# A spectral mixer and MLP on one core: staging places, conversion slots and output buffers changed

## The chip, the cores and the metric

The kernel runs on one core of a Trainium2 chip. The metric is the device time of one execution in microseconds (us), the median of three runs. Engines are called TensorE (PE in the rows, with its weight loads as PEld), VectorE (DVE), ScalarE (ACT), GpSimd (POOL) and SyncE (SP, which issues nearly all DMAs here).

## What is computed

Eight sequences of 3072 tokens with 256 channels go through a real FFT along the sequence, a complex 256 x 256 mix with bias, a soft threshold of 0.01 and the inverse FFT, and then through an MLP with 2048 hidden units and a softplus.

```python
X = np.fft.rfft(x, axis=1)
Yr = Xr @ w_r - Xi @ w_i + b_r
Yi = Xr @ w_i + Xi @ w_r + b_i
Yr = np.sign(Yr) * np.maximum(np.abs(Yr) - 0.01, 0.0)     # Yi the same
y = np.fft.irfft(Y, n=3072, axis=1)
h = y.reshape(-1, 256) @ w_in
g = np.maximum(h, 0.0) + np.log1p(np.exp(-np.abs(h)))
out = g @ w_out
```

Matrix products are made of three: each operand is split into a high part and a remainder, and high x high, high x remainder and remainder x high are summed. The MLP weights arrive as 64-bit numbers and are converted on the chip.

## The kernel before

**Order.** Everything is issued in an order that the program writes out itself (`manual_schedule`). The end of the function is a planner and a loop over slots. `product(i, f, ...)` puts one step of the spectral part into the first free slot from i on, `at(i, f, ...)` puts DMA issues and small work into slot i, `before` holds the weight conversions, whose pieces go one to a slot. In each slot the loop emits, in this order: the first half of the MLP's products (`slot_products`), one piece of each running conversion, the spectral step, the `at` list, whatever was put off in the slot before (`later`: stores and remainders), and the second half of the products (`slot_second`). Each engine runs its own instructions strictly in that order. A tile that is asked for when all buffers of its tag hold tiles in use makes its first writer wait for one of them.

**Slots.** Slots -64 to -1 are the fill: the whole spectral part of batch 0, up to its first pair of token blocks. From slot 0 on, four slots make one key (b, bp, mp): batch, pair of token blocks (three to a batch), and one of eight double tiles of the hidden units. Eight keys, 32 slots, make a pair; 768 slots in all. A plain slot has twelve matmuls and takes 2.72 us with nothing waiting, the third of each four nine and 2.04. Into these slots go the spectral steps of the batches to come: s1 (0.69 us of TensorE), s3 (0.91), mix (2.17), s4 (0.68), s5 (1.37). `add(key, C11, "e")` and `add(key, C21, "e")` on VectorE free the PSUM bank "e" that the first matmul of the next slot's `pse` group overwrites.

**Turns.** Only the first two pairs (0,0) and (0,1) take turns: each runs half of its hidden units (slots 0 to 15 and 16 to 31), puts its sums into DRAM (`part_dr`), and comes back for the other half (32 to 47 and 48 to 63) so that there is time to convert the second half of the weights. `load_part` brings the sums back. In a pair's last but one and last steps (the second and third slot after its 32, called e+1 and e+2 with e the next pair's first slot) `ffn2` copies four [128 x 512] results from PSUM into `ot` tiles: block j=1 in e+1, block j=0 in e+2, each with k=0 on ScalarE and k=1 on VectorE, and stores them one slot later. When partial sums are added, VectorE makes all four.

**Buffers in question.** Tag "ot" (2 buffers) holds the four results and, during conversions, the work tile `u`. Tag "d" (2 buffers) holds the results of s4 on their way to DRAM (`s4`, line 434, stored one slot later). "r0" and "r1" hold the raw tokens of s5. "dp" (4) holds s5's inputs and early raw weights; "w64" (1) later raw weights; "wp" (1) the converted weights before they are stored to DRAM, from where `stream_w` reads them for each key.

**Conversions.** Sixteen of them (w_in and w_out by turns, eight double tiles). Six start in the fill ("ahead", their adds on GpSimd), in slots -42 to -7, seven slots apart; the others start in slots 0, 3, 6, 10, ... 34.

Of the kernel before, what the change touches and what calls it, by code (L numbers as in the profile page):

```python
# [10 lines left out]
F32 = mybir.dt.float32  # L11
F32R = mybir.dt.float32r
# [5 lines left out]
P = 128  # L18
N1, N2 = 96, 32
NG = 24  # L20
NP = NG // 2
BLK = 512
# [11 lines left out]
def tile_spectral_mixer_mlp(ctx, tc, x, w_r, w_i, bias, bias_0, w_in, w_out, f, f_hi, f_lo, g1, g3, g3_hi, g3_lo, hm, out):  # L34
# [14 lines left out]
    sb = ctx.enter_context(tc.tile_pool(name="sb", bufs=2))  # L49
# [23 lines left out]
    w_1 = y1[:, 10 * 512:].bitcast(F32R)  # L73
# [23 lines left out]
    def store(dst, src, what, eng=None):  # L97

        def start():
            (eng or nc.sync).dma_start(dst, src)  # L100
            stored[what] += 1

        later.append(start)
# [32 lines left out]

    def load_w(which, m2):

        if m2 < 3:
            st = sb.tile([P, 1024 + 4 * N1], F32, tag="dp", name="w64", bufs=4)[:, :1024]  # L140
        else:
            st = sb.tile([P, 1024], F32, tag="w64", name="w64", bufs=1)
        nc.sync.dma_start(st.rearrange("p (a n) -> p a n", a=2).bitcast(U32), (w_in if which else w_out)[:, m2])
        stages[which, m2] = st

    def split_w(which, m2):

        st = stages.pop((which, m2)).bitcast(U32).rearrange("p (n w) -> p n w", w=2)
        lw, hw = st[:, :, 0], st[:, :, 1]
        t = sb.tile([P, 512], F32, tag="t", name="wt", bufs=5)
        u = sb.tile([P, 512], F32, tag="ot", name="wu")
        ti, ui = t.bitcast(U32), u.bitcast(U32)
        v, g = nc.vector, nc.gpsimd
        nc.scalar.activation(u, hw.bitcast(F32), AF.Square)
        v.tensor_scalar(out=ti, in0=hw, scalar1=3, scalar2=0x3FFFFFF8, op0=ALU.logical_shift_left, op1=ALU.bitwise_and)
        v.scalar_tensor_tensor(out=ti, in0=hw, scalar=0xC0000000, in1=ti, op0=ALU.bitwise_and, op1=ALU.bitwise_or)  # L160
        nc.scalar.mul(lw.bitcast(F32), lw, 2.0 ** -52)
        yield
        v.scalar_tensor_tensor(out=t, in0=u, scalar=2.0 ** -30, in1=t, op0=ALU.is_ge, op1=ALU.mult)
        v.tensor_scalar(out=ui, in0=ti, scalar1=0xFF800000, scalar2=None, op0=ALU.bitwise_and)
        g.tensor_tensor(out=u, in0=lw.bitcast(F32), in1=u, op=ALU.mult)
        yield
        n = 7 * P if which else 2 * D
        w = w_1 if early and which else sb.tile([P, 2 * 7 * P], F32R, tag="wp", name="wp", bufs=1)
        w = w[:, :2 * n]
        hi, lo, src = w[:, :n], w[:, n:], w[:, n:].bitcast(F32)  # L170
        ahead = bool(early)
        e = g if ahead else v
        if which:

            tm, um = [a.rearrange("p (k m n) -> p m k n", k=2, m=2) for a in (t, u)]
            a21 = tm[:, 1, 0]
            o = [src[:, i * P:(i + 1) * P] for i in range(7)]
            e.tensor_tensor(out=src[:, A11 * P:(A11 + 2) * P].rearrange("p (k n) -> p k n", k=2), in0=tm[:, 0], in1=um[:, 0], op=ALU.add)
            e.tensor_tensor(out=a21, in0=a21, in1=um[:, 1, 0], op=ALU.add)
            e.tensor_tensor(out=o[A22], in0=tm[:, 1, 1], in1=um[:, 1, 1], op=ALU.add)  # L180
        else:
            e.tensor_tensor(out=src, in0=t, in1=u, op=ALU.add)
        if ahead:
            yield
            yield
        if which:
            v.tensor_tensor(out=o[S1], in0=a21, in1=o[A22], op=ALU.add)
            v.tensor_tensor(out=o[S3], in0=o[A11], in1=a21, op=ALU.subtract)
            v.tensor_tensor(out=o[S2], in0=o[S1], in1=o[A11], op=ALU.subtract)
            v.tensor_tensor(out=o[S4], in0=o[A12], in1=o[S2], op=ALU.subtract)  # L190
        yield
        nc.scalar.copy(hi, src)
        yield
        v.tensor_tensor(out=lo, in0=src, in1=hi.bitcast(F32), op=ALU.subtract)
        yield
        nc.sync.dma_start((w1_dr if which else w2_dr)[m2][:, :], w.bitcast(F32))
        stored["w", which, m2] += 1
# [10 lines left out]
    def mm3(ps, wh, wl, xh, xl, start, stop, more=False):  # L208
        nc.tensor.matmul(ps, wh, xh, start=start, stop=False, skip_group_check=more)  # L209
        nc.tensor.matmul(ps, wh, xl, start=False, stop=False, skip_group_check=more)  # L210
        nc.tensor.matmul(ps, wl, xh, start=False, stop=stop, skip_group_check=more)  # L211
# [10 lines left out]
    early = [None]  # L222
# [376 lines left out]
    def load_part(blk):  # L599
        partial[blk] = []  # L600
        for k in range(2):
            assert stored["part", blk, k] == 1
            t = sb.tile([P, BLK], F32, name="part", **(dict(tag="d") if blk % 2 else dict(tag=f"r{k}", bufs=1)))
            nc.sync.dma_start(t, part_dr[blk, k][:, :])
            partial[blk].append(t)

    def ffn2(key, what, first, last):
        b, bp, mp = key
        m, j = divmod(what, 2)
        blk = 2 * bp + j  # L610
        if first:
            po[b, blk] = [ps_o.tile([P, BLK], F32, tag="o", name="pso") for _ in range(2)]
        wt = w_t[0, key].rearrange("p (h n) -> p h n", h=2)
        gh, gl = gt.pop((key, what))
        for k in range(2):
            w = slice(m * D + k * P, m * D + k * P + P)
            mm3(po[b, blk][k], wt[:, 0, w], wt[:, 1, w], gh, gl, first, last)
        if last:
            o = po.pop((b, blk))
            for k in range(2):  # L620
                ot = sb.tile([P, BLK], F32, tag="ot", name="ot")
                if blk in partial and not b:
                    nc.vector.tensor_tensor(out=ot, in0=o[k], in1=partial[blk][k], op=ALU.add)
                elif k == 0:
                    nc.scalar.copy(ot, o[k])
                else:
                    nc.vector.tensor_copy(ot, o[k])
                if mp == NM // 2 - 1:
                    store(out[b, blk, k], ot, "out")
                else:  # L630
                    part_dr[blk, k] = dram.tile([P, BLK], F32, tag=f"part{blk}{k}", name="part_dr", bufs=1)
                    store(part_dr[blk, k][:, :], ot, ("part", blk, k))
# [51 lines left out]
    with tc.manual_schedule():  # L684
# [7 lines left out]
        def at(i, f, *args):  # L692
            fill.setdefault(int(i), []).append((f, args))

        def product(i, f, *args):
            i = int(i)
            while i in steps:
                i += 1
            steps[i] = f, args
            return i  # L700

        def plan_s1(b, start, step, first=0):
            for c in range(first, 16):
                t = product(start + step * (c - first), s1, b, c)
                at(t - 3, split_x, b, c)
                at(t - (5 if b == 1 else 7), load_x, b, c)

        def plan_mix(b, start, step):
            mixed = done = start
            for gp in range(NP):  # L710
                t = product(max(start + step * gp, mixed), s3, b, gp)
                at(max(t - 4, 14), load_a, b, gp)
                mixed = product(max(t + (3 if gp else 4), done + 1), mix, b, gp)
                done = product(mixed + (3 if b == 1 else 4), s4, b, gp)

        def plan_s5(b, bp, start):

# [21 lines left out]
        t0 = -len(first)  # L739
# [18 lines left out]
            at(t0 + 14 + k, load_mix, k)  # L758
            at(t0 + 18 + k, split_mix, k)
        for j in range(NM):  # L760
            t = t0 + 22 + 7 * j if j < 6 else 3 * (j - 6) if j < 8 else 6 + 4 * (j - 8)
            at(t - (6 if j < 6 else 8 if j < 7 else 2), load_w, (j + 1) % 2, j // 2)
            before.setdefault(t, []).append(split_w((j + 1) % 2, j // 2))
        last = first.index(("s4", 0, NP - 1)) + t0
        for c in need_d(0):
# [6 lines left out]
            at(6 + 2 * k, combine_mix, 1 + k)  # L772

        nt = NT
        plan_s1(1, 0, 1.6, 8)
        for b in range(B):
            for bp in range(1, NPAIR):
                plan_s5(b, bp, nt * b + (NM if (b, bp) == (0, 1) else 2 * NM * bp) - 14)
            if b + 1 < B:
                plan_mix(b + 1, *((16, 4.9) if b == 0 else (nt * b - 4, 5.6)))  # L780
                plan_s5(b + 1, 0, nt * (b + 1) - 14)
        for b in range(2, B):
            plan_s1(b, *((16, 4.4) if b == 2 else (nt * (b - 2) - 4, 5.4)))
# [2 lines left out]
        for bp in range(2):  # L786
            t = 4 * keys.index((0, bp, NM // 2 - 1))
            at(t + 4, load_part, 2 * bp + 1)
            at(t + 5, load_part, 2 * bp)
        for i, key in enumerate(keys):  # L790
            if i:
                at(4 * i - 4, stream_w, 1, key[2], key)
# [5 lines left out]
        for i in range(min([*fill, *steps]), nt * B + 3):  # L798
# [8 lines left out]
            if i in steps:  # L807
                f, args = steps.pop(i)
# [108 lines left out]
```

## Time and profile before

| | us |
|---|---|
| median of three runs (2702.85 to 2706.63) | 2703.62 |
| the profiled execution | 2708.39 |
| its span, from first to last instruction | 2706.2 |
| TensorE busy in the span | 2616.3 (97%) |
| VectorE, ScalarE, GpSimd busy | 1635.0, 1725.3, 298.0 |

Where slots begin in this trace, found by counting the groups of six `pso` matmuls that end each slot:

| slot | begins at us | slot | begins at us |
|---|---|---|---|
| 0 | 124.4 | 40 | 324.0 |
| 12 | 196.7 | 52 | 366.0 |
| 21 | 238.75 | 53 | 377.1 |
| 36 | 297.7 | 76 | 474.5 |

A busy TensorE is no measure of speed by itself, since its clock has two levels; the granted clock stands beside the busy time (1.00 is the full 2.4 GHz, 0.50 is 1.2 GHz). Idle time in brackets is that of the engine just before the instruction, with what ended it.

### The profile page before, as it was taken

How to read it: one execution, taken by the hardware profiler on the slowest of the kernel's cores; microseconds unless marked ns; L12 is line 12 of the kernel's file. 1: busy time of each engine (PE TensorE's matmuls, PEld its weight loads, DVE VectorE, ACT ScalarE, POOL GpSimd, SP SyncE). 2: the span in 40 equal slices, each digit the busy share in tenths (PEclk: the TensorE clock that was granted, in tenths of full speed). 3: DMA queues.
4: the chain of work that ended last, by engine and by line, in shares of the span. 5: the costliest groups of instructions: out<-in, count | busy, mean ns of one | idle time of the engine just before them, and what ended most of it. 6: DMA issues, size and time to landing. Idle time of an engine off the chain costs nothing.

```text
span 2706.2 us, 36340 instructions
## 1 busy us (share of the span) xinstructions
PE 2616.3 (97%) x13061; PEld 2192.6 (81%) x13061; DVE 1635.0 (60%) x2716; ACT 1725.3 (64%) x3118; POOL 298.0 (11%) x287
## 2 busy tenths in 40 slices
PE   7878898999999999999999999999999999999999
PEld 5656677888888888888888888888888888888887
DVE  3657666566656666466665666656765666644554
ACT  3456555666666666666666666666666666666665
POOL 2332101101101101011011010110010000000000
PEclk8888899999999999999999999999999999999999
DMA  5756564565464654555655655546555455445543
GB/s 184 242 191 220 195 194 154 183 212 164 150 216 162 198 173 161 185 181 178 200 169 177 205 165 176 178 163 208 175 164 192 163 168 186 144 155 176 181 148 114
DMA packets 188420, 483.93 MB, mean 179 GB/s; under 512 B 18352, under 2 KB 87216, under 8 KB 188240
## 3 DMA queue, kind: packets, MB, share of 16 engines
q1 hardware_dynamic: 187680, 481.14, 55.0%
q8 instruction: 103, 1.69, 0.3%
q0 software_dynamic: 560, 0.47, 0.1%
q14 instruction: 77, 0.63, 0.1%
HBM read 392.41 MB, written 85.98 MB: 177 GB/s over the span
## 4 chain that ended last, share of the span: by engine, by line
PE 81%; DVE 1%; ACT 1%; DMA 1%; issue 0%; SPq 0%; DVEq 0%
PE pso L209 12%; PE pso L211 12%; PE pso L210 12%; PE psc L209 6%; PE psc L211 6%; PE psc L210 6%; PE pse L209 4%; PE pse L211 4%; PE pse L210 4%; PE psf L457 4%; PE psf L210 3%; PE psf L209 3%; PE psf L211 3%; PE psf L289 2%; DVE shrunk L415 0%; DMA out_y<-ot 0%
## 5 line engine op out<-in xcount | busy, mean ns | idle before, releaser
L583 DVE TENSOR_TENSOR gl<-t,gh 128x512 fp32r<-128x512 f32 x768 | 536.3, 698 | 333.6 <-ACT gh L577 330.7
L567 DVE TENSOR_TENSOR t<-pse,t 128x512 f32<-128x512 f32 x576 | 396.1, 688 | 437.0 <-ACT t L562 284.1
L562 ACT COPY t<-psc 128x512 f32<-128x512 f32 x576 | 337.8, 586 | 480.6 <-PE psc L211 478.7
L209 PE MATMUL pso<-gh,w 128*128 128x512 f32 x1536 | 616.6, 401 | 0.0
L210 PE MATMUL pso<-gl,w 128*128 128x512 f32 x1536 | 600.5, 391 | 0.0
L211 PE MATMUL pso<-gh,w 128*128 128x512 f32 x1536 | 600.5, 391 | 0.0
L577 ACT CAST gh<-t 128x512 fp32r<-128x512 f32 x768 | 477.2, 621 | 78.2 <-PE pso L211 54.8
L573 ACT ACTIVATE t<-t 128x512 f32<-128x512 f32 x576 | 364.4, 633 | 80.6 <-DVE t L567 79.8
L211 PEld LDWEIGHTS pso<-gh,w 128*128 128x128 f32 x1536 | 289.2, 188 | 62.5
L209 PEld LDWEIGHTS pso<-gh,w 128*128 128x128 f32 x1536 | 290.4, 189 | 55.1
L210 PEld LDWEIGHTS pso<-gl,w 128*128 128x128 f32 x1536 | 290.4, 189 | 51.5
L209 PE MATMUL psc<-y_sb,w 128*128 128x512 f32 x768 | 303.2, 395 | 23.5 <-ACT t L562 19.0
L211 PE MATMUL psc<-y_sb,w 128*128 128x512 f32 x768 | 301.6, 393 | 0.0
L210 PE MATMUL psc<-y_sb,w 128*128 128x512 f32 x768 | 301.0, 392 | 0.0
L209 PE MATMUL pse<-y_sb,w 128*128 128x512 f32 x576 | 229.9, 399 | 29.2 <-DVE t L567 29.2
L115 POOL TENSOR_TENSOR xl<-xt,xh 96x512 fp32r<-96x512 f32 x104 | 138.5, 1333 | 931.1 <-ACT xh L106 783.6
L210 PE MATMUL pse<-y_sb,w 128*128 128x512 f32 x576 | 226.5, 393 | 0.0
L211 PE MATMUL pse<-y_sb,w 128*128 128x512 f32 x576 | 226.4, 393 | 0.0
L494 POOL TENSOR_TENSOR y_sb<-raw,y_sb 128x512 fp32r<-128x512 f32 x69 | 92.6, 1343 | 1134.5 <-ACT y_sb L491 1123.7
L209 PEld LDWEIGHTS psc<-y_sb,w 128*128 128x128 f32 x768 | 145.1, 189 | 58.3 <-ACT t L562 21.6
L211 PEld LDWEIGHTS psc<-y_sb,w 128*128 128x128 f32 x768 | 145.4, 189 | 31.3
L210 PEld LDWEIGHTS psc<-y_sb,w 128*128 128x128 f32 x768 | 145.4, 189 | 29.8
(138 smaller groups left out, 3648.3 us busy)
## 6 DMA issues: line engine op xcount, KB each, us to landing
w<-w_dr SPq DMA_DIRECT2D x192, 896.0 KB
w<-w_dr SPq DMA_DIRECT2D x192, 512.0 KB
dp<-d_dr SPq DMA_DIRECT2D x80, 384.0 KB
xt<-in_x SPq DMA_DIRECT2D x128, 192.0 KB
d_dr<-d SPq DMA_DIRECT2D x96, 256.0 KB
out_y<-ot SPq DMA_DIRECT2D x96, 256.0 KB
ap<-a_dr SPq DMA_DIRECT2D x84, 256.0 KB
a_dr<-a SPq DMA_DIRECT2D x104, 192.0 KB
```

The costliest lines, as they stand in the source:

```text
L115: (eng or nc.vector).tensor_tensor(out=lo, in0=src, in1=hi.bitcast(F32), op=ALU.subtract)
L209: nc.tensor.matmul(ps, wh, xh, start=start, stop=False, skip_group_check=more)
L210: nc.tensor.matmul(ps, wh, xl, start=False, stop=False, skip_group_check=more)
L211: nc.tensor.matmul(ps, wl, xh, start=False, stop=stop, skip_group_check=more)
L289: nc.tensor.matmul(xv[:, g, k], t[:, g, k * P:(k + 1) * P], g1_t[:, g].rearrange("p (c s) -> p c s", c=2), start=True, stop=True,)
L457: nc.tensor.matmul(ps[:, t - blk * BLK:t - blk * BLK + n], d_sb[b, blk // 2, n2 // 4][0][:, n2 % 4, k * P:(k + 1) * P], d_sb[b, blk // 2, ...
L494: eng.tensor_tensor(out=lo, in0=raw[j], in1=hi.bitcast(F32), op=ALU.subtract)
L562: nc.scalar.copy(t, banks[bank])
L567: nc.vector.tensor_tensor(out=t, in0=banks[bank], in1=t, op=ALU.add)
L573: nc.scalar.activation(t, banks[bank] if bank else t, AF.Softplus)
L577: nc.scalar.copy(gh, ct[key, what])
L583: nc.vector.tensor_tensor(out=gl, in0=ct.pop((key, what)), in1=gh.bitcast(F32), op=ALU.subtract)
```

## The change

The raw weights always go into "dp" (no "w64"); the space is used for a second staging place, "wq" for w_out beside "wp" for w_in. Eight conversions start in the fill, in slots -40, -35, -30, -25, -20, -14, -9 and -4; none starts in slots 0 to 11; the other eight start in slots 12, 15, ... 33 (three slots apart), their loads three slots earlier. Both blocks of partial sums come back into r0 and r1, block j=0 one slot later than before (slot e+2). The results of block j=0 go into tag "d", those of j=1 stay in "ot", and this in all 24 pairs. The steps s1 of batch 1 are put 1.4 slots apart rather than 1.6, its s3 and mix steps 4.8 rather than 4.9 apart, and its s4 four slots after the mix rather than three (the last one in slot 80 rather than 75). The plan of batches 2 to 7 is the same in both.

```diff
--- before.py
+++ after.py
@@ -136,10 +136,7 @@
 
     def load_w(which, m2):
 
-        if m2 < 3:
-            st = sb.tile([P, 1024 + 4 * N1], F32, tag="dp", name="w64", bufs=4)[:, :1024]
-        else:
-            st = sb.tile([P, 1024], F32, tag="w64", name="w64", bufs=1)
+        st = sb.tile([P, 1024 + 4 * N1], F32, tag="dp", name="w64", bufs=4)[:, :1024]
         nc.sync.dma_start(st.rearrange("p (a n) -> p a n", a=2).bitcast(U32), (w_in if which else w_out)[:, m2])
         stages[which, m2] = st
 
@@ -165,8 +162,7 @@
         g.tensor_tensor(out=u, in0=lw.bitcast(F32), in1=u, op=ALU.mult)
         yield
         n = 7 * P if which else 2 * D
-        w = w_1 if early and which else sb.tile([P, 2 * 7 * P], F32R, tag="wp", name="wp", bufs=1)
-        w = w[:, :2 * n]
+        w = w_1[:, :2 * n] if early and which else sb.tile([P, 2 * n], F32R, tag=("wq", "wp")[which], name="wp", bufs=1)
         hi, lo, src = w[:, :n], w[:, n:], w[:, n:].bitcast(F32)
         ahead = bool(early)
         e = g if ahead else v
@@ -600,7 +596,7 @@
         partial[blk] = []
         for k in range(2):
             assert stored["part", blk, k] == 1
-            t = sb.tile([P, BLK], F32, name="part", **(dict(tag="d") if blk % 2 else dict(tag=f"r{k}", bufs=1)))
+            t = sb.tile([P, BLK], F32, name="part", tag=f"r{k}", bufs=1)
             nc.sync.dma_start(t, part_dr[blk, k][:, :])
             partial[blk].append(t)
 
@@ -618,7 +614,7 @@
         if last:
             o = po.pop((b, blk))
             for k in range(2):
-                ot = sb.tile([P, BLK], F32, tag="ot", name="ot")
+                ot = sb.tile([P, BLK], F32, tag=("d", "ot")[j], name="ot")
                 if blk in partial and not b:
                     nc.vector.tensor_tensor(out=ot, in0=o[k], in1=partial[blk][k], op=ALU.add)
                 elif k == 0:
@@ -711,7 +707,7 @@
                 t = product(max(start + step * gp, mixed), s3, b, gp)
                 at(max(t - 4, 14), load_a, b, gp)
                 mixed = product(max(t + (3 if gp else 4), done + 1), mix, b, gp)
-                done = product(mixed + (3 if b == 1 else 4), s4, b, gp)
+                done = product(mixed + 4, s4, b, gp)
 
         def plan_s5(b, bp, start):
 
@@ -758,8 +754,8 @@
             at(t0 + 14 + k, load_mix, k)
             at(t0 + 18 + k, split_mix, k)
         for j in range(NM):
-            t = t0 + 22 + 7 * j if j < 6 else 3 * (j - 6) if j < 8 else 6 + 4 * (j - 8)
-            at(t - (6 if j < 6 else 8 if j < 7 else 2), load_w, (j + 1) % 2, j // 2)
+            t = t0 + 24 + 26 * j // 5 if j < 8 else 12 + 3 * (j - 8)
+            at(t - (6 if j < 8 else 3), load_w, (j + 1) % 2, j // 2)
             before.setdefault(t, []).append(split_w((j + 1) % 2, j // 2))
         last = first.index(("s4", 0, NP - 1)) + t0
         for c in need_d(0):
@@ -772,12 +768,12 @@
             at(6 + 2 * k, combine_mix, 1 + k)
 
         nt = NT
-        plan_s1(1, 0, 1.6, 8)
+        plan_s1(1, 0, 1.4, 8)
         for b in range(B):
             for bp in range(1, NPAIR):
                 plan_s5(b, bp, nt * b + (NM if (b, bp) == (0, 1) else 2 * NM * bp) - 14)
             if b + 1 < B:
-                plan_mix(b + 1, *((16, 4.9) if b == 0 else (nt * b - 4, 5.6)))
+                plan_mix(b + 1, *((16, 4.8) if b == 0 else (nt * b - 4, 5.6)))
                 plan_s5(b + 1, 0, nt * (b + 1) - 14)
         for b in range(2, B):
             plan_s1(b, *((16, 4.4) if b == 2 else (nt * (b - 2) - 4, 5.4)))
@@ -786,7 +782,7 @@
         for bp in range(2):
             t = 4 * keys.index((0, bp, NM // 2 - 1))
             at(t + 4, load_part, 2 * bp + 1)
-            at(t + 5, load_part, 2 * bp)
+            at(t + 6, load_part, 2 * bp)
         for i, key in enumerate(keys):
             if i:
                 at(4 * i - 4, stream_w, 1, key[2], key)
```

## Rows read from the trace of the kernel before

**Rows 1.** The page's slices: busy tenths, granted clock, 40 equal slices of the span

```profile
PE   7878898999999999999999999999999999999999
...
PEclk8888899999999999999999999999999999999999
```

**Rows 2.** Stretches by time: length, then busy us (xinstructions) of each engine, clock, DMA

```profile
124.40:196.70 72.30, 50.05 (x192) 37.47 (x192) 41.41 (x70) 41.12 (x75) 24.18 (x17) 0.77 0.61 191
196.70:238.75 42.05, 32.93 (x138) 26.20 (x137) 27.62 (x48) 22.55 (x40) 11.88 (x14) 0.84 0.69 233
238.75:297.70 58.95, 54.53 (x280) 44.86 (x278) 50.91 (x96) 41.87 (x77) 8.95 (x6) 1.00 0.63 216
297.70:324.00 26.30, 17.94 (x70) 14.02 (x71) 15.22 (x26) 11.00 (x21) 2.58 (x3) 0.74 0.49 169
...
366.00:377.00 11.00, 5.25 (x16) 3.73 (x15) 4.73 (x8) 2.95 (x5) 0.00 (x0) 0.69 0.85 289
377.00:475.00 98.00, 90.66 (x463) 76.70 (x462) 61.71 (x104) 57.20 (x104) 11.54 (x9) 0.95 0.48 154
```

**Rows 3.** VectorE in order of time, five waits: start, length, line [idle before <-releaser]

```profile
168.34 0.69 DVE L182 TENSOR_TENSOR wp<-wt,wu 128x512 f32<-128x512 f32 x1 [13.29 <-DMA w_dr<-wp]
...
229.81 0.69 DVE L627 COPY ot<-pso 128x512 f32<-128x512 f32 x1 [7.38 <-DMA part_dr<-ot]
...
304.11 0.69 DVE L627 COPY ot<-pso 128x512 f32<-128x512 f32 x1 [9.06 <-DMA part_dr<-ot]
...
370.08 1.31 DVE L623 TENSOR_TENSOR ot<-pso,part 128x512 f32<-128x512 f32 x2 [6.08 <-DMA out_y<-ot]
...
439.44 0.69 DVE L623 TENSOR_TENSOR ot<-pso,part 128x512 f32<-128x512 f32 x1 [5.93 <-DMA out_y<-ot]
```

**Rows 4.** TensorE in order of time, two gaps

```profile
171.30 0.79 PE L209 MATMUL psc<-y_sb,w 128*128 128x512 f32 x1 [13.00 <-ACT t L562]
...
372.65 0.80 PE L209 MATMUL pse<-y_sb,w 128*128 128x512 f32 x1 [5.75 <-DVE t L567]
```

**Rows 5.** SyncE's DMA issues in order of time, at a pair's turn, slot 19

```profile
223.35 0.85 SPq L205 DMA_DIRECT2D w<-w_dr  x1
224.29 6.56 SPq L100 DMA_DIRECT2D part_dr<-ot  x2
```

**Rows 6.** TensorE at a later pair's end, slots 130 to 132

```profile
655.00 0.39 PE L209 MATMUL psf<-sh,g3h 128*128 128x512 f32 x1
...
657.04 0.39 PE L209 MATMUL psc<-y_sb,w 128*128 128x512 f32 x1
...
662.62 0.39 PE L209 MATMUL pse<-y_sb,w 128*128 128x512 f32 x1
```

**Rows 7.** VectorE at the same pair's end

```profile
659.30 0.69 DVE L627 COPY ot<-pso 128x512 f32<-128x512 f32 x1 [2.79 <-PE psf L211]
...
661.05 0.68 DVE L567 TENSOR_TENSOR t<-pse,t 128x512 f32<-128x512 f32 x1
```

**Rows 8.** SyncE's DMA issues at the same pair's end

```profile
657.23 0.38 SPq L205 DMA_DIRECT2D w<-w_dr  x1
657.70 0.38 SPq L100 DMA_DIRECT2D d_dr<-d  x1
```

**Rows 9.** TensorE at the next pair's end, slots 163 and 164

```profile
770.58 0.39 PE L209 MATMUL psc<-y_sb,w 128*128 128x512 f32 x1
...
774.68 0.39 PE L209 MATMUL pse<-y_sb,w 128*128 128x512 f32 x1
```

**Rows 10.** VectorE's last instruction

```profile
2702.21 0.69 DVE L627 COPY ot<-pso 128x512 f32<-128x512 f32 x1 [2.19 <-DMA out_y<-ot]
```

**Rows 11.** Conversions on VectorE, groups by shape: busy, mean ns

```profile
L160 DVE SCALAR_TENSOR_TENSOR wt<-w,wt 128x512 uint32<-128x512 uint32 x16 | 12.1, 758 | 0.5
...
L182 DVE TENSOR_TENSOR wp<-wt,wu 128x512 f32<-128x512 f32 x5 | 5.6, 1118 | 13.3 <-DMA w_dr<-wp 13.3
```

**Rows 12.** One stretch of the fill, columns as in rows 2

```profile
50.00:75.00 25.00, 25.00 (x183) 22.38 (x183) 22.29 (x37) 11.01 (x22) 11.31 (x8) 1.00 0.55 190
```

## The prediction

> **What bounds the kernel now.** I read the page's slices first. From the ninth of 40 on, TensorE is busy in nine tenths or more and its clock is granted in full; only the first eight slices hold sevens and eights [rows 1]. So TensorE bounds the kernel, some 85 us excepted, and these lie in the first 475 us. To place them I took the windows by time and cut them at the slots of the table: a stretch's length, less TensorE's busy time times its granted clock (work at full speed), is what it loses. Slots 0 to 11: 72.30 − 50.05 x 0.77 = 33.8 us. Slots 12 to 20: 42.05 − 32.93 x 0.84 = 14.4. Slots 21 to 35: 58.95 − 54.53 = 4.4. Slots 36 to 39: 26.30 − 17.94 x 0.74 = 13.0. Slot 52: 11.00 − 5.25 x 0.69 = 7.4. Slots 53 to 75: 98.00 − 90.66 x 0.95 = 11.9 [rows 2]. Together 84.9 us; more than that can't be won in these stretches.
>
> Then the waits, VectorE's first, since TensorE's gaps end on tiles that VectorE or ScalarE fill. In slot 6 VectorE waits 13.29 us for a store of wp, and TensorE stands still for 13.00. Its four other long waits, 7.38, 9.06, 6.08 and 5.93 us, are copies or sums into ot that wait for an older ot to be stored [rows 3]; the third of them is a TensorE gap of 5.75 [rows 4]. That gap is most of slot 52, which lost 7.4: a stall costs 7.4 / 5.75 = 1.29 times its length, the rest being matmuls at the lower of the clock's two levels behind it. I use 1.29 wherever a gap is turned into time.
>
> **The change, part by part.** Slots 0 to 11 (no conversion there any more): the wait on wp goes, with the pieces of four conversions. Of 33.8 us the gap with its clock is 13.00 x 1.29 = 16.8, and some more is pieces crowding VectorE (41.41 of 72.30 us). Late next are s1's token loads and ScalarE's 41.12 us [rows 2], which I can't see ending a wait. Bounds −10 (only the gap shortened to what a late token load leaves) and −27 (four fifths of the loss); I take **−20**, a little over the gap.
>
> Slots 12 to 20: block j=0 of the first turn finds free d tiles, so VectorE's 7.38 [rows 3] goes. But eight conversions now start three slots apart, not four; each puts at least four pieces of 0.76 to 1.12 us on VectorE [rows 11], 3.0 to 4.5 us in 8.2 us of slots. A staging place is asked for again only six slots later, at least two slots after its store is issued. The u of a conversion still holds an ot, so a ScalarE copy can still wait. Bounds 0 and −12, taken **−8**.
>
> Slots 21 to 39: VectorE is already busy 50.91 of 58.95 us [rows 2] and gets about one conversion more. At the turn after slot 32 a u still holds one of the two ot, and the new s4 of slot 34 holds one of the two d, so part of the 9.06 wait stays. Bounds +8 (the wait moves, VectorE fills up) and −10, taken **−2**.
>
> Slots 40 to 75: the two ends at 48 and 64 lose 7.4 and 11.9. Partial sums of j=1 come into r0 and r1; sums of j=0 are loaded a slot later into the same two, so this load waits for VectorE's adds of j=1 and lands, at 5.52 us (below), some 1.4 us after it is wanted, once per end. The waits of 6.08 and 5.93 go. 19.3 − 2 x 1.4 x 1.29 = 15.7 would be all but that. Bounds −8 and −19, taken **−16**.
>
> Fill: two conversions more start before slot 0. In the stretch read there TensorE is busy 25.00 of 25 and VectorE 22.29 [rows 12]: 2.7 us are free on VectorE in 25, and two conversions want 6.0 to 9.0 there; GpSimd makes their adds. Bounds −1 (they fall into idle parts) and +12 (all eight to nine us on the path with the clock), taken **+6**.
>
> Last pair: the last copy waited 2.19 us for a store of ot [rows 10]; it goes into a free d: **−1.5**, between 0 and −2.2.
>
> Batches 1 to 6, new: block j=0 takes d in every pair, and d is also s4's. In twelve of their pairs (two to a batch, which carry the s4 of the batch to come) an s4 lies in the very slot e+2 in which j=0 is copied; one such end is slot 130 [rows 6]. There s4 takes one of the two d, the k=0 copy the other, and the k=1 copy, on VectorE, has to wait for s4's d_dr store. That is issued in the next slot: with E the start of slot e+3, at E + 0.66 (657.70 − 657.04), behind a load of weights at 657.23 [rows 6, 8]. Its landing is not in the rows. Nearest is the part_dr pair, issued likewise behind a w load, at 224.29, whose wait ended at 229.81: 5.52 us [rows 3, 5]. Ends: 2.19 in the quiet tail [rows 10], and 9.06, the longest such wait [rows 3]. I take 5.52, since queue and order are the same. The tile is free at E + 6.18 and the 0.69 us copy done at E + 6.87. Behind it on VectorE queue the t additions and remainders, and TensorE's first products of the new pair overwrite the bank that the copy empties; their second group starts 1.36 us ahead of the next slot's pse, so at 662.62 − 1.36 = E + 4.22 where a mix lies between [rows 6], and at 774.68 − 1.36 = E + 2.74 where none does [rows 9]. Six ends are of either sort: stalls of 2.65 and 4.13 us, 6 x 6.78 = 40.7 us, and with the clock x 1.29 **+52**. With 2.19 it would be 6 x 0.8 = +5; with 9.06 it would be 83, or 107 with the clock. The 2.79 us that VectorE waited in this place before cost TensorE nothing [rows 7], since ot's stores were issued a slot earlier.
>
> The Trainium skill ("DMA: Bandwidth & Descriptors", Latency and other measured facts) puts a DMA's fixed cost at about 2 us, mostly the trip to the memory and back. Alone that would have the store land like the tail's, and the +52 would be +5 and the change faster. The same page (Queues, rings and completion order) has each ring served in order, and by that a store behind half a megabyte of weights waits for these; the 5.52 us agree with the second.
>
> Seven further ends have s4 two slots later (slot e+4), where ScalarE may wait a little for the k=0 result's store: 0 to +1 each, taken 0, as a mix follows. All other edits (s1 and mix of batch 1 a little closer or later) stay within stretches counted above: 0.
>
> Sum: −20 − 8 − 2 − 16 + 6 − 1.5 + 52 = +10.5. The profiled execution took 2708.39 us (span 2706.2, 2.2 around it), 4.8 above the median; as a difference the sum goes onto the median: 2703.62 + 10.5 = 2714.
>
> **The rivals.** First: the d_dr store lands early. If it lands in 2.2 to 3 us, the late ends cost +5 and the rest stays: −41.5 + 5 = −36.5, so 2667 (2655 to 2690). For it: 256 KB is small and the queue was shared with few others; 2.19 was measured for out_y [rows 10]. Against: the tail had no weight loads, these ends have one just ahead [rows 8]. It decides from a landing of about 3 us downwards. The page's 2 us is this case. Chance 0.18, all of it faster.
>
> Second: the clock pays for long stalls only. The late gaps of 2.65 and 4.13 are shorter than any whose clock the rows show; if it stays at its upper level there, they cost 41, and if the early stretches likewise come back in full (−27, −12, −10, −19, −2.2, with +6 in the fill) the sum is −23: 2680 (2668 to 2705). For it: all late slices show a full clock [rows 1]. Against: VectorE's load in slots 21 to 35 stays [rows 2]. Chance 0.15: 0.12 faster, 0.03 same.
>
> Third: VectorE becomes the bound where the conversions now lie, or the second staging place doesn't take the waits away there, since stores of a conversion land as late as the 13.29 says. Then the fill costs 12, slots 12 to 20 give 3, slots 21 to 39 lose 8: 6 + 5 + 10 = 21 us more than the forecast, 2735 (2724 to 2750). For it: 22.29 of 25 [rows 12] and 50.91 of 58.95 [rows 2]. Against: the pieces before were no denser than one in four slots and TensorE lost only 4.4 in slots 21 to 35. Chance 0.20: 0.18 slower, 0.02 same.
>
> **How the numbers follow.** The forecast, 2714 with a range of its own of 2704 to 2728 (landings of 5 to 6.5 us), has the remaining 0.47. About 0.2%, 5.4 us, is what a measurement of this kernel can tell from no change, so 2698 to 2709 is "same": 0.13 of the forecast's chance lies there, 0.34 above. Faster 0.18 + 0.12 = 0.30; same 0.13 + 0.03 + 0.02 = 0.18; slower 0.34 + 0.18 = 0.52. The range reaches from the first rival's centre to a third of the way above the third's: 2667 to 2742; about 0.1 is left out on either side.
>
> **What would show it.** In the profile after: no wait on w_dr in slots 0 to 11 and slot 12 beginning some 20 us sooner, counted from slot 0; slot 0 beginning about 6 us later; near slots 48 and 64 gaps of a microsecond or two only. In the slices, eights among the nines of the later part, twelve of them; at each of these ends a VectorE copy into d with a wait of four us or so, released by d_dr<-d, and right after it a TensorE gap of 2.6 or 4.1 before a pso or pse group. If these waits last a microsecond, the first rival holds. If the gaps are there but the clock doesn't fall, the second. If slots 12 to 39 take longer than before with VectorE full, the third. What I may have wrong altogether is the order in which d's two buffers come free: were the k=1 copy to wait for an older tile, no late stall would exist.

## The result

The changed kernel takes 2727.69 us (median of four, 2719.84 to 2733.29), the kernel before 2705.12 over its four runs: a ratio of 1.0082, interval 1.0055 to 1.0109. It is slower, by 22.6 us. The forecast was 2714, slower, with a range of 2667 to 2742.

Two profiled executions are set side by side here: spans of 2725.3 and 2706.2 us, a difference of 19.1. First the page's slices, and the chain of work that ended last with its share by engine and line, both of the changed kernel.

```profile
PE   7788899999999999999999999999999999999999
...
PEclk8899999999999999999999999999999999999999
...
PE pso L205 12%; PE pso L206 12%; PE pso L207 12%; PE psc L205 6%; PE psc L207 6%; PE psc L206 6%; PE pse L205 5%; PE psf L453 5%; PE pse L206 5%; PE pse L207 5%; PE psf L205 3%; PE psf L206 3%; PE psf L207 3%; DMA d_dr<-d 2%; PE psf L285 2%
```

Beside [rows 1] the clock is in the nines from the third slice on and not from the sixth, and TensorE's busy digits are higher in two of the early slices (the third and the seventh) and lower in one: the stretch that lost 85 us did improve. The late slices are nines in both, since a slice is 68 us and a stall of 3 us disappears in it: the slices don't show where the time went. The chain does. Its last but one entry, stores of d with 2% of the span (some 54 us, as far as a rounded share tells), is not in the list of the kernel before.

TensorE's waits in sum, columns: waiting group and releaser, us in total, times, longest. Kernel after first, then the same line of before.

```profile
PE pse L205 <- DVE t L563: 57.5, 33, 5.7
```
```profile
PE pse L209 <- DVE t L567: 29.2, 18, 7.4
PE psc L209 <- ACT t L562: 19.0, 5, 13.0
```

The wait of 13.0 is gone after, and TensorE's waits on VectorE before a pse group have grown from 18 to 33. The places follow from the slots: in the kernel after, slot 0 begins at 126.6 us, 12 at 180.1, 21 at 220.7, 36 at 289.9, 40 at 308.4, 53 at 356.6, 76 at 440.4. The stretches of [rows 2], cut at the same slots (the fourth begins at slot 36, the fifth is slot 52):

```profile
126.60:180.10 53.50, 44.40 (x180) 34.90 (x180) 23.15 (x35) 32.75 (x60) 15.54 (x14) 0.83 0.69 214
180.10:220.70 40.60, 31.25 (x151) 25.91 (x150) 30.17 (x55) 25.12 (x45) 12.51 (x15) 0.92 0.71 242
220.70:289.90 69.20, 58.81 (x272) 47.14 (x271) 55.55 (x100) 44.63 (x80) 14.89 (x9) 0.93 0.61 209
289.90:308.40 18.50, 14.53 (x61) 11.53 (x60) 13.53 (x24) 10.62 (x19) 0.01 (x1) 0.91 0.57 197
351.00:356.60 5.60, 3.66 (x16) 2.66 (x15) 4.96 (x10) 3.17 (x7) 0.00 (x0) 1.00 0.90 317
356.60:440.40 83.80, 83.65 (x441) 71.17 (x441) 57.43 (x98) 56.37 (x104) 12.03 (x9) 1.00 0.55 183
```

Slots 0 to 11 take 53.5 us instead of 72.3, slots 12 to 20 40.6 instead of 42.05, slots 21 to 39 87.7 instead of 85.25, and slots 53 to 75 now run without loss. Up to slot 84 the changed kernel is 31.2 us ahead. It loses all of that and 20.7 more between slots 100 and 700, nearly all of it in twelve places. Two of them, VectorE's waits first (each line an instruction: start, length, line [idle before <-releaser]), at slots 131 and 163:

```profile
632.53 0.69 DVE L623 COPY ot<-pso 128x512 f32<-128x512 f32 x1 [7.18 <-DMA out_y<-ot]
...
748.44 0.69 DVE L623 COPY ot<-pso 128x512 f32<-128x512 f32 x1 [5.70 <-DMA d_dr<-d]
```

SyncE's issues at these two ends:

```profile
626.07 0.57 SPq L201 DMA_DIRECT2D w<-w_dr  x1
626.73 0.38 SPq L100 DMA_DIRECT2D d_dr<-d  x1
...
743.46 0.33 SPq L201 DMA_DIRECT2D w<-w_dr  x1
743.88 0.39 SPq L100 DMA_DIRECT2D d_dr<-d  x1
```

TensorE there:

```profile
634.47 0.50 PE L205 MATMUL pse<-y_sb,w 128*128 128x512 f32 x1 [2.85 <-DVE t L563]
...
750.38 0.50 PE L205 MATMUL pse<-y_sb,w 128*128 128x512 f32 x1 [2.85 <-DVE t L563]
```

Before, at the first of these ends, VectorE waited 2.79 us and TensorE didn't wait for it [rows 6, 7]. Now the copy begins 5.80 and 4.56 us after the d_dr store was issued, the additions queue behind it, and TensorE's pse waits 2.85 us for one of them. (Eight of the twelve waits name d_dr; three, this first one too, name out_y, the store issued right behind it, and one ScalarE.)

### The profile page after: what moved, and what is told of

The parts are those of the page before. It is cut to its first block, busy times and chain, and to the rows that moved or that the text cites. A ratio compares the mean times of both kernels' runs of the same rounds, so it can differ in the third digit from the quotient of the medians.

```text
span 2725.3 us, 36405 instructions
## 1 busy us (share of the span) xinstructions
PE 2619.5 (96%) x13061; PEld 2197.2 (81%) x13061; DVE 1630.1 (60%) x2712; ACT 1728.4 (63%) x3118; POOL 302.9 (11%) x291
## 4 chain that ended last, share of the span: by engine, by line
PE 85%; DMA 6%; DVE 5%; issue 2%; ACT 1%; SPq 1%; POOL 0%; DVEq 0%; ACTq 0%; POOLq 0%
PE pso L205 12%; PE pso L206 12%; PE pso L207 12%; PE psc L205 6%; PE psc L207 6%; PE psc L206 6%; PE pse L205 5%; PE psf L453 5%; PE pse L206 5%; PE pse L207 5%; PE psf L205 3%; PE psf L206 3%; PE psf L207 3%; DMA d_dr<-d 2%; PE psf L285 2%
## 5 line engine op out<-in xcount | busy, mean ns | idle before, releaser
L563 DVE TENSOR_TENSOR t<-pse,t 128x512 f32<-128x512 f32 x576 | 396.2, 688 | 440.8 <-ACT t L558 289.9
L207 PEld LDWEIGHTS pso<-gh,w 128*128 128x128 f32 x1536 | 289.9, 189 | 63.0
L205 PEld LDWEIGHTS pso<-gh,w 128*128 128x128 f32 x1536 | 291.7, 190 | 55.3
L206 PEld LDWEIGHTS pso<-gl,w 128*128 128x128 f32 x1536 | 291.4, 190 | 51.6
L205 PEld LDWEIGHTS pse<-y_sb,w 128*128 128x128 f32 x576 | 109.5, 190 | 94.4 <-DVE t L563 72.3
L205 PEld LDWEIGHTS psc<-y_sb,w 128*128 128x128 f32 x768 | 145.0, 189 | 48.6 <-ACT t L558 9.3
L207 PEld LDWEIGHTS psc<-y_sb,w 128*128 128x128 f32 x768 | 145.0, 189 | 31.2
```

What stands on the lines that cost most here:

```text
L563: nc.vector.tensor_tensor(out=t, in0=banks[bank], in1=t, op=ALU.add)
```

## The experiments

The theory: the late loss is twelve waits of the k=1 copy for an s4's store, in tag d. The rival: it comes from something else in the change. Four runs first.

**d for the results of batch 0 only.**

```
-                ot = sb.tile([P, BLK], F32, tag=("d", "ot")[j], name="ot")
+                ot = sb.tile([P, BLK], F32, tag="ot" if j or b else "d", name="ot")
```

> The changed kernel, with the results of block j=0 in tag d only in batch 0 and in ot again in batches 1 to 7. Theory (the k=1 copy waits for the d_dr store of an s4 in the same slot, at twelve pair ends): the late part, which lost 52 us against the kernel before between slots 128 and 700, loses nothing; 2727.7 - 52 = 2676 us (2668 to 2684), and no VectorE wait on d_dr after slot 100. Rival (the late loss comes from elsewhere in the change, such as SBUF places or the clock after a denser start): 2715 or more.

Measured 2678.42 us (2672.95 to 2682.47), 0.9905 of the kernel before, interval 0.9885 to 0.9925. TensorE's waits on VectorE fall back, below those of before:

```profile
PE pse L205 <- DVE t L563: 21.5, 21, 5.2
```

From slot 100 to 760 its trace takes 2129.7 us; the kernel before 2127.3, the changed kernel 2179.0. The rest of the change thus wins 27 us and this one line costs 49.

**The same line alone, in the kernel before.**

```
-                ot = sb.tile([P, BLK], F32, tag="ot", name="ot")
+                ot = sb.tile([P, BLK], F32, tag="ot" if j or not b else "d", name="ot")
```

> The kernel before, with one part of the change alone: block j=0 in tag d in batches 1 to 7. Theory: the twelve pair ends cost here what they cost in the changed kernel, +52: 2705 + 52 = 2757 us (2748 to 2766), slots 0 to 100 as before. Rival (the late loss needs the rest of the change): 2705 to 2712.

Measured 2760.2 us (2757.36 to 2764.98), ratio 1.0215 (1.0196 to 1.0234), so +55: the cost needs nothing else of the change. VectorE's waits by releaser, where the kernel before has no such line for d_dr:

```profile
DVE ot L627 <- DMA d_dr<-d: 63.2, 10, 7.3
```

**s4 a slot earlier.**

```
-                done = product(mixed + 4, s4, b, gp)
+                done = product(mixed + (3 if b > 1 and gp in (5, 11) else 4), s4, b, gp)
```

> The changed kernel, with the s4 steps 5 and 11 of batches 2 to 7 three slots after their mix and not four, so in slot e+1 and not e+2; d for j=0 stays. Theory: the store of s4 is issued one slot (2.7 us) earlier, its tile is free at about E + 3.8 and the copy done at E + 4.5; due at E + 4.2 (six ends) and E + 2.7 (six): stalls of 0.3 and 1.8, 13 us, with the clock 16 rather than 52: 2692 us (2678 to 2700). Rival (two users of d within a pair's end cost as much wherever the s4 lies): 2720 to 2730.

Measured 2704.09 us (2700.12 to 2708.45): outside both. The plan shows why: with s4 of step 5 earlier the steps behind it move too, and in the end the mix of step 11 comes a slot later (159 instead of 158), so that its s4, three slots behind it, stays in slot e+2 (162). The run therefore holds both cases, six ends each. Its copies at the ends of slots 128 and 160:

```profile
632.72 0.69 DVE L623 COPY ot<-pso 128x512 f32<-128x512 f32 x1
...
747.09 0.69 DVE L623 COPY ot<-pso 128x512 f32<-128x512 f32 x1 [5.66 <-DMA d_dr<-d]
```

and the stretches around them (columns as in the stages above):

```profile
617.00:640.00 23.00, 23.00 (x118) 19.34 (x117) 18.66 (x34) 16.86 (x32) 1.29 (x1) 1.00 0.63 206
733.00:755.00 22.00, 19.20 (x72) 15.07 (x71) 11.91 (x20) 13.46 (x24) 2.83 (x2) 0.85 0.58 192
```

With s4 in e+1 the copy doesn't wait and TensorE loses nothing; with s4 in e+2, in the same run, VectorE waits 5.66 us, TensorE loses 2.8 and its clock falls to 0.85. About half of the loss gone (24 of 49 us) is what the edit, as the planner carried it out, had to give. The miss was in reading my own edit, and the second theory of that run, that two users of d cost as much anywhere, falls.

**The stores ahead of the load.** In slot e+3 the put-off stores are issued before the load of w_out.

```
+            if i > 96 and i % 32 == 3:
+                for _ in range(due):
+                    later.popleft()()
+                due = 0
             for f, args in fill.pop(i, ()):
                 f(*args)
```

> The changed kernel, with the stores put off from slot e+2 issued ahead of the load of w_out (512 KB) in slot e+3 of the pairs of batches 1 to 7, so ahead of it on SP's queue and not behind it. Theory A (the store lands late because it stands behind the load): it lands about 2.5 us after its issue at E + 0.2, the copy is done at E + 3.4, stalls 0 and 0.7 us at six ends each, 4 us, with the clock 5: 2727.7 - 47 = 2681 us (2672 to 2692). Theory B (4.5 to 6 us is the store's own time at this load): only the 0.5 us of an earlier issue is won, twelve times 0.5 with the clock 7: 2720 us (2714 to 2726).

Measured 2677.76 us (2676.72 to 2681.38), as theory A: d stays, s4 stays in e+2, and the loss is gone but for a small rest. SyncE and VectorE at the end of slot 160:

```profile
740.01 0.38 SPq L100 DMA_DIRECT2D d_dr<-d  x1
...
743.47 0.88 SPq L201 DMA_DIRECT2D w<-w_dr  x2
```
```profile
742.32 0.69 DVE L623 COPY ot<-pso 128x512 f32<-128x512 f32 x1 [2.29 <-PE psf L205]
```

The store was issued at 740.01, and by 742.32 at the latest, 2.3 us later, its tile was free. (The wait that is left names TensorE here; at seven of the twelve ends it names d_dr.) Behind the load the same took 4.56 us at this end, so some 2.2 us of it was the place on the queue. This end is one of the quick ones: from the store's issue to the copy the run takes 2.3 to 3.0 us at seven ends, where the changed kernel took 4.5 to 4.8, and 3.6 to 4.1 at the other five, where it took 5.8 to 6.1. Being first, the store is also issued 1.2 us sooner, 0.55 us before slot e+3 begins instead of 0.61 after. In the trace the twelve ends together cost 3.2 us against the kernel before; in the changed kernel they cost 50.8.

The other four concern the first 450 us.

**One staging place**, everything else as in the run with d in batch 0 only:

```
-        w = w_1[:, :2 * n] if early and which else sb.tile([P, 2 * n], F32R, tag=("wq", "wp")[which], name="wp", bufs=1)
+        w = w_1 if early and which else sb.tile([P, 2 * 7 * P], F32R, tag="wp", name="wp", bufs=1)
+        w = w[:, :2 * n]
```

> As the run with d for j=0 in batch 0 only (2678 us), but with one staging place wp for w_in and w_out, as in the kernel before, under the new conversion slots. Theory (both parts are needed: no conversions in slots 0 to 11 removes the 13.29 us wait, and the second place lets them follow three slots apart later): from slot 17 on each of seven conversions asks for wp in the slot in which its store is issued and waits about 5 us for the landing; 7 x 5 with the clock 45: 2723 us (2705 to 2740), slots 0 to 12 unchanged at 53.7 us. Rival (the new slots alone bring the gain): 2676 to 2684.

Measured 2681.19 us (2680.14 to 2682.69; the run it departs from 2678.42): the rival. VectorE's waits for wp's store:

```profile
DVE wp L179 <- DMA w_dr<-wp: 7.6, 3, 3.1
```

Three waits of at most 3.1 us, where seven of 5 were expected. So the second staging place is worth at most a few us, and the gain of the early slots came from the rest of the change there: most likely from the conversions' starts, since no piece of one runs in slots 0 to 11 any more (the raw weights in "dp" and the new slots of their loads weren't tried apart). Nor was a wait of 13.29 [rows 3] the price of a second visit to wp as such. SyncE's issues just before it in the kernel before, then one of the three stores that were waited for here, with the instruction that waited:

```profile
156.60 0.38 SPq L205 DMA_DIRECT2D w<-w_dr  x1
157.03 0.61 SPq L100 DMA_DIRECT2D a_dr<-a  x1
157.74 0.41 SPq L196 DMA_DIRECT2D w_dr<-wp  x1
```
```profile
258.29 0.33 SPq L193 DMA_DIRECT2D w_dr<-wp  x1
...
263.05 0.69 DVE L179 TENSOR_TENSOR wp<-wt,wu 128x512 f32<-128x512 f32 x1 [3.06 <-DMA w_dr<-wp]
```

In the kernel before, 2.7 us of the wait had passed when the store was issued, behind a load of weights, and 10.6 us more went by until the tile was free, at 168.34. Here the three stores were issued with nothing on the queue just ahead of them, and their tiles were free after 4.5 to 4.9 us. That fits the place on the queue once more, but no run moved that store alone.

**No d for results at all** (tag "ot" for every result):

> As the run with d for j=0 in batch 0 only (2678 us), but with ot for all results in batch 0 too. Theory (d takes a VectorE wait for a part_dr store off the turns, as the forecast had it): the copies of j=0 at slots 18, 34, 50 and 66 wait again for stores issued a slot later; two to four stalls of 2 to 5 us, +8 to +20: 2692 us (2684 to 2700). Rival (in slots 12 to 39 d only moves the wait to the conversion's u and to s4's store, and at 50 and 66 the waits stay hidden): 2674 to 2682.

Measured 2682.48 us (2681.48 to 2684.38), 4 more than with d in batch 0, between the two and nearer to the rival. Its copies wait as before the change, and the kernel with d shows what is left without these waits. VectorE without d, at the turns of slots 16 and 32, then ScalarE at the first of them:

```profile
209.14 0.69 DVE L623 COPY ot<-pso 128x512 f32<-128x512 f32 x1 [9.10 <-DMA part_dr<-ot]
...
279.14 0.69 DVE L623 COPY ot<-pso 128x512 f32<-128x512 f32 x1 [6.19 <-DMA part_dr<-ot]
...
290.37 0.69 DVE L623 COPY ot<-pso 128x512 f32<-128x512 f32 x1 [7.88 <-DMA part_dr<-ot]
```
```profile
204.81 0.66 ACT L155 ACTIVATE wu<-w 128x512 f32<-128x512 f32 x1 [6.60 <-DMA part_dr<-ot]
```

The changed kernel at the same turns, ScalarE, then VectorE:

```profile
209.39 0.66 ACT L155 ACTIVATE wu<-w 128x512 f32<-128x512 f32 x1 [6.60 <-DMA part_dr<-ot]
```
```profile
281.77 0.69 DVE L623 COPY ot<-pso 128x512 f32<-128x512 f32 x1 [5.50 <-DMA part_dr<-ot]
...
292.50 0.69 DVE L623 COPY ot<-pso 128x512 f32<-128x512 f32 x1 [7.38 <-DMA d_dr<-d]
```

At the first turn d takes VectorE's 9.10 us wait away, but ScalarE waits 6.60 us with d and without it, where u of the conversion that starts in slot 18 wants an ot, and TensorE's gap behind that in slot 20 stays: 7.06 us without d, 7.07 with it (before the change 2.71 and 4.36, in two gaps). At the second, 6.19 and 7.88 became 5.50 and 7.38, for ot with u in slot 33, and for d with s4 in slot 34.

**No d, and the pace of batch 1 as before** (s1 1.6 apart, s3 and mix 4.9, s4 three slots after the mix):

> As the run without d for results, and with s1, s3, mix and s4 of batch 1 at the pace of the kernel before. Theory (the denser s1 makes ScalarE wait 6.43 us in slots 2 and 3 for a token load that is queued behind eight loads for s5, since its slot comes sooner): slot 4 begins about 5 us sooner after slot 0, and s4 three slots after its mix costs at most 2: 4 us faster than the run without d. Rival (the token load is as late at either pace): within 2 us of it in slots 0 to 12.

Measured 2683.51 us (2682.55 to 2689.07), as much as without. In slots 0 to 11 (49.2 us, against 50.9 without) ScalarE's token wait is 5.45 us instead of 6.87 and TensorE's gap behind it 4.69 instead of 7.30: a part of what was expected. TensorE's gap is clear of the runs at 1.4 (6.2 to 8.7 us in eight traces), the 1.7 us of the stretch less so: slots 0 to 11 take 50.9 to 55.3 us in the traces of runs that are alike there. What was won is lost again by slot 84 (345.1 us from slot 0, against 343.9): in slots 23, 27 and 31 TensorE waits 2.89, 2.36 and 1.26 us for remainders (sl) that s4 now asks for a slot sooner. The pace moves time about; as a whole it wins none.

**Stores ahead of the loads at every pair's end**, the first turns too (the condition becomes `i > 0 and i % 16 == 3`, which takes in slot 3 and a slot in the middle of each pair as well):

> The changed kernel with the put-off stores ahead of the loads in slots 19, 35, 51, 67 too, so that at every pair's end stores go ahead of the load of w_out. Theory: the 7.38 us wait for d_dr at the turn after slot 32 becomes 2 to 4 us, which takes some 5 us off slots 33 to 36 (20.2 us long), slots 16 to 20 keep their wait since it is u's: 2677.8 - 5 = 2673 us (2668 to 2677). Rival (at that turn VectorE's conversion pieces set the time, not the store): 2676 to 2681.

Measured 2675.7 us (2671.15 to 2680.63), where 2673 was expected and 2677.76 the run without: within their spread, so the verdict is open by the medians. At the turn itself the traces tell more. VectorE's copy in the run without, then the store and the same copy in this one:

```profile
290.76 0.69 DVE L623 COPY ot<-pso 128x512 f32<-128x512 f32 x1 [7.28 <-DMA d_dr<-d]
```
```profile
280.95 0.45 SPq L100 DMA_DIRECT2D d_dr<-d  x1
...
285.06 0.69 DVE L623 COPY ot<-pso 128x512 f32<-128x512 f32 x1 [4.55 <-DMA d_dr<-d]
```

TensorE's gap behind it in slot 36 falls from 4.55 to 0.55 us, and slots 33 to 36 take 25.4 us instead of 29.7 (the 20.2 of the expectation are slots 33 to 35). There the theory holds, in one trace each; the four traces with the loads first at this turn, and conversions and d alike, have 29.4 to 30.4.

**Conversions off the turns**, on top of it:

```
-            t = t0 + 24 + 26 * j // 5 if j < 8 else 12 + 3 * (j - 8)
+            t = t0 + 24 + 26 * j // 5 if j < 8 else (12, 15, 20, 21, 24, 27, 30, 36)[j - 8]
```

> The changed kernel with the stores ahead of the loads at all pair ends (2675.7 us, its profiled run some 5 below that), and conversions started in slots 12, 15, 20, 21, 24, 27, 30, 36 instead of 12, 15, 18, 21, 24, 27, 30, 33, so that no work tile u is asked for or held while a turn's copies need both ot. Theory (the 6.60 us ScalarE wait in slot 18 and the 5.4 us VectorE wait at the turn after slot 32 both come from u in tag ot, and hold TensorE for 7.06 and 5.61): slots 16 to 20 give back 5 to 9, slots 33 to 36 4 to 7: 2663 us (2656 to 2669). Rival (two conversions close together, or the last one later, crowd VectorE instead): 2672 to 2680.

Measured 2665.37 us (2662.82 to 2665.54). Slots 16 to 20, from the run before and from this one:

```profile
187.20:216.40 29.20, 19.87 (x93) 16.37 (x92) 21.34 (x43) 15.60 (x28) 7.50 (x12) 0.88 0.63 213
```
```profile
187.70:207.70 20.00, 17.73 (x93) 14.88 (x93) 19.00 (x35) 14.69 (x27) 5.53 (x11) 1.00 0.73 246
```

9.2 us, and the conversion moved from slot 18 to 20, with its load, is all that differs there: the work tile u did hold the turn of slot 16. At the turn of slot 32 (slots 33 to 37) only 2.3 us came back, 29.7 to 27.4: VectorE no longer waits for an ot there, but still for the s4's d, 9.55 us.

```profile
265.81 0.39 SPq L100 DMA_DIRECT2D d_dr<-d  x1
...
274.92 0.69 DVE L623 COPY ot<-pso 128x512 f32<-128x512 f32 x1 [9.55 <-DMA d_dr<-d]
```

That store was ahead of the loads of its slot, as in the run before, and yet its tile was free only 9.1 us after its issue, not 4.1. In both runs a conversion's store was issued 0.4 us ahead of it. What differs in the traces is what the DMA engines had left to do: from 265.4 to 270.0 they are 0.98 busy here, while in the run before, where TensorE had stood 5.6 us until 278.50, they are 0.18 busy from 276.0 to 280.5, just before the store. So being ahead of the load seems not to be enough where earlier transfers still run; no run tests this alone.

**The old pace of s1 on top of that** (1.6 slots):

> The run before this one (starts off the turns), with s1 of batch 1 put 1.6 slots apart again. Theory (with s1 closer, its token load is wanted sooner after the eight loads for s5, and ScalarE waits 6.4 us for it; the old pace gave slots 0 to 12 in 49.2 us rather than 53.5): 4 us less than that run, all in slots 0 to 12. Rival (the 4 us came from the other changes of pace, or are lost again in slots 12 to 36): within 2 us of it, or more.

Measured 2660.9 us (2658.7 to 2663.92), 0.983 of the kernel before (0.9817 to 0.9844). The 4.5 us by the medians are as expected, but the traces don't bear them out: the two profiled executions took 2663.92 and, in the run before, 2662.82 us. Of the expected cause they show a part: ScalarE still waits 6.64 us for the tokens (7.51 in the run before), TensorE 4.58 behind it instead of 7.94, and slots 0 to 11 take 50.35 us instead of 51.6. The intervals of the two ratios overlap, so what the pace is worth stays open. It is the fastest version found by the medians, 45 us below the kernel before and 67 below the changed one.

## Why the prediction came out

The direction and the place of the new cost were right, and its mechanism but for the last link. Its price came out by two errors that offset each other, which is luck. Of the early terms the two large ones were right, and the forecast was too kind in the middle. Term by term, in the profiled executions (slot times of the two traces):

| term | forecast | measured |
|---|---|---|
| fill, up to slot 0 | +6 | +2.2 |
| slots 0 to 11 | −20 | −18.8 |
| slots 12 to 20 | −8 | −1.5 |
| slots 21 to 39 | −2 | +2.5 |
| slots 40 to 75 | −16 | −18.4 |
| slots 76 to 83 | 0 | +2.9 |
| twelve ends with an s4 in e+2 | +52 | +50.8 |
| all else from slot 84 to the last copy | 0 | +0.9 |
| last copies | −1.5 | −1.5 |
| sum | +10.5 | +19.1 |

**The twelve ends.** The forecast took a landing of 5.52 us from a row of another place, [rows 5], because order and queue were alike; the two ends shown have 5.80 and 4.56, five of the twelve 5.8 to 6.1 and seven 4.5 to 4.8. The last link was another than forecast. The new pair's products were to wait for the bank that the copy empties; they didn't, their second group began before the copy, which started at 632.53:

```profile
630.09 0.40 PE L205 MATMUL pso<-gh,w 128*128 128x512 f32 x1
```

TensorE stands at the next slot's pse instead, whose bank an addition frees that stands behind the copy on VectorE. Counted by that path, the forecast's landing gives stalls of 2.4 and 3.9 us, near its 2.65 and 4.13, so the wrong link cost the sum little. Stalls with the clock were to cost 3.4 us at ends with a mix and 5.3 without; over six ends each they cost 22.6 and 28.2 us, 3.8 and 4.7. Of the sum, 50.8, TensorE's idle time has 35.9 (forecast 40.7) and slower matmuls 14.9: 1.42 times the idle time, not 1.29. So the term came out because the stalls were shorter and the clock dearer than taken. Nor does each end pay for the clock. Slots 160 to 167 and 448 to 455 of the changed kernel (columns as in the stages above):

```profile
735.11:760.74 25.63, 22.79 (x100) 18.35 (x99) 12.56 (x18) 16.61 (x29) 2.95 (x2) 1.00 0.61 194
1717.71:1746.28 28.57, 25.70 (x100) 20.44 (x99) 12.95 (x18) 16.62 (x29) 2.58 (x2) 0.88 0.53 172
```

Both hold one gap, of 2.85 and 2.87 us, and in the kernel before both stretches took 22.49. The granted clock stays at 1.00 in the first and falls to 0.88 in the second; at six of the twelve ends it falls (to 0.88 to 0.94 over eight slots), and matmuls take 1.4 to 3.2 us more, at the other six it is 1.00 and they take 0.3 to 0.6 more. What decides between the two isn't shown. So the second rival, in which the clock stays up behind short gaps, was right at half of the ends and wrong at the other half.

The first rival (a landing of 2.2 us) had about the price that the store has when it isn't behind the load: the run with stores first shows 2.3 to 3.0 us at seven ends, 3.6 to 4.1 at five, and next to no loss. So this rival had nearly the right figure for another order of the queue. The Trainium skill's figure of about 2 us ("DMA: Bandwidth & Descriptors", Latency and other measured facts) is near those seven, with the store at the head of the queue. That each ring is consumed in order, as the Trainium skill has it (the same title, Queues, rings and completion order), agrees with the 4.5 to 6.1 us of the store behind half a megabyte.

**Slots 0 to 11** gave what the forecast took, though for half a reason. The gap of 13.00 with its clock, 16.8 us, went, and a new one came: ScalarE waits 6.43 us for tokens in slot 2 and TensorE 6.80 behind it, the late token load that the forecast named as next in line but gave no price. VectorE has less to do there besides, 23.15 us instead of 41.41; what that alone is worth no run shows. Of the 18.8 us, 1.4 are an s5 that the new plan puts into slots 12 to 20, where it is missing from the gain. The second staging place had no part in it that the runs could show.

**Slots 12 to 39** is the step that failed: −10 forecast, +1.0 measured, more than the 8.6 us that separate the two sums. The forecast named both mechanisms (a conversion's u in ot that makes ScalarE wait, an s4 in slot 34 that holds a d) and then priced them as remainders. They were nearly the whole: in slot 20 TensorE stood 7.07 us behind ScalarE's wait of 6.60, as long as in its two gaps before the change, and the turn of slot 32 kept its 5.50 and 7.38. The run with conversions off the turns gives 9.2 us back from the first of them alone.

**Slots 40 to 75** came out near the end of the forecast's bounds (−19): of TensorE's waits one of 1.94 us is left at slot 52 and none at 68. Whether that one comes from the shared r0 and r1, as the forecast had it, isn't shown: VectorE's first sum of j=0 there waits 1.41 us, and the profile names a TensorE group that had ended 0.7 us before. **Slots 76 to 83** were counted nowhere: batch 1's steps end five slots later, in slot 80, and bring work along that the kernel before had done by then: one mix and one s4, 2.17 and 0.68 us, which the slots before 76 no longer hold, so it is no cost of the change. **The fill** cost 2.2 of the 6 taken in these two traces; that is within what traces of one and the same fill differ by (slot 0 begins at 123.7 to 128.8 us in the ten traces with the new fill, at 121.4 and 124.4 with the old one). Ends with s4 in e+4 are six and not seven, as the plan's slots show: three cost 0.4 to 0.5 us each and three nothing, within the 0 to +1 that was bounded.

The execution that the forecast was read from (2708.39) was 4.8 above the median of before; the changed kernel's runs spread over 13 us. The 22.6 us of the medians and the 19.1 of the traces differ by no more than that.

## What to carry to other kernels

Giving a result another tag to free it from its own wait makes it a partner in that tag's timetable: list who else asks for the tag in the same slot, and when the older tile's store is issued. With a few us of slack per block, what is issued first on the queue (a store that frees a buffer, or a half-megabyte load that isn't needed for four slots) decided 50 us here, for no change in the work. And look for such stalls in the sums of waits and in the chain: a slice of 1/40 of the span shows nothing of a 3 us stall every 100 us.

## What was unexpected of the hardware

The wait for the 896 KB store of a conversion was 13.29 us in slot 6 and at most 3.1 us with the same single staging place in later slots, where nothing stood just ahead of the store. A wait's length was a poor estimate for the same store at another place on the queue, while a wait at a like place (5.52 for 4.5 to 6.1) was a good one. And a gap of TensorE of the same length, 2.85 us, was followed by a lower clock at some pair ends and by the full clock at others.
